# Two more first-layer units by seven products in chunks 2 and 3 of a fused attention and two-layer kernel

## The chip, the cores and the metric

The kernel runs on one core of a Trainium2 chip. The metric is the device time of one execution in microseconds. Before the change it is 325.47 us, the median of 3 runs (325.46 to 325.6). The engines are called PE (matrix products; PEld is its loading of weights), DVE (vector), ACT (activations), POOL (GpSimd) and SP (queue of transfers).

## The reference

Attention with a forgetting gate over 8 batches of 8 heads, 576 tokens and 64 values a head; its output, 4608 tokens of 512 values, goes through two layers with a gelu (tanh form) between them.

```
scores = q k^T / sqrt(64) + (cum[i] - cum[j]),  cum = cumsum(log(clip(f, 1e-4, 1)))
attn   = softmax over j <= i of scores;   x = attn v, heads side by side: 4608 x 512
out    = gelu_tanh(x @ w_in) @ w_out      w_in 512 x 2048, w_out 2048 x 512
```

## The kernel before

**Tiles.** A quad is four heads of one batch; there are 16, numbered 0 to 15, two in each batch. `xT` holds the attention output transposed, 512 values by 4608 tokens, and is filled by quads. The two layers go over the tokens in nine chunks (0 to 8) of 512. `gT` holds the gelus of the chunk at work.

**Stages.** FRONT, a string of words, covers the loads, quads 0 to 5, the layers of chunk 0 and most of chunk 1. Then TABLES[c] is played for chunks 2 to 8: first the rest of the chunk before (`O`), the first layer, and then the second layer woven with the attention of quads 2c+2 and 2c+3 and the first scores of 2c+4. In a table `q2` means quad 2c+2, and so on. The order is written by hand: each word issues its instructions to their engines, and each engine works through its own queue in that order.

**Words of attention** (a number after the dot is the quad). LK, LQ: load k, q on POOL's queue into one of two buffers (L192); LV: load values on SP's queue. TK, TQ: transpose them on DVE (L198). S.i.r: scores of round r on PE (L261) and their exponentials on ACT into `pt` (L269). M: causal masks by select on POOL (L275); m: masks by a product on DVE (L304). A last number picks the key block, so m.5.2.2 is quad 5, round 2, block 2. D: denominators on PE with the weights `w_bf` (L329), then two transposes and a reciprocal on DVE (L348 to L352). V.i.x: a half of the output on PE (L329) and its product on DVE into `xT` (L360). VW and vw: weighted values on POOL or DVE (L215). CL: copies a block of them (L220). D and V share one PSUM tile, `po`, which the DVE instruction behind each gives free. X and Y load the tables of ACT. D takes the key blocks in the order 0, low, 1, 2, 3, high.

**First layer.** P.n computes a pair of 128-row tiles of the 16 directly: 16 matmuls of 512 columns (L374) and one gelu (L381). P.n.1 takes the tile `po` for it. A unit by seven products (R.k, three words to a unit: `seven_in`, L412) computes the pairs k and k+4 together: seven products of 2 x 2 matmuls of 256 columns (L422), six sums and copies on DVE (L435 to L452), four gelus on ACT (L431). It takes two tiles `s` and both tiles `m` of PSUM. It needs four sums of the weights (K.k, L410; three are kept in the columns of an old chunk of `xT`, that of HOMES, the fourth, K.k.3, overwrites a part of `w_in_sb`) and four differences of the inputs (T, L395), which are kept in the columns of the chunk before in `xT`. So K.k.3 comes after the last direct use of these weights. In a table T makes the differences for the next chunk.

**Second layer.** G makes the sums of `gT` on DVE (L489 to L495). F and f pull so many of its 112 matmul steps (L510; f in four column strips). Its sums are L535 on DVE, its stores go on SP's queue.

**Units before.** Chunk 2 has no unit, chunk 3 one (k = 1), chunks 4 to 8 two (k = 1 and 3). All K are made in chunk 2, but for K.3.3 in chunk 3. Chunk 1 is played in the last three lines of FRONT (L80 to L82), with G.0, G.1.1.2 and the F and f of chunk 1; there V.4.1, CL.5 and m.5.2.2 stand next to each other, ahead of D.5.

Of the kernel before, what the change touches and what calls it, by code (L numbers as in the profile page):

```python
# [16 lines left out]
def kernel(  # L17
# [10 lines left out]
    nc = tc.nc  # L28

    B, H, S, D = q.shape  # L30
# [47 lines left out]
        J.0.2 J.1.2 X LK.4 F.0.6 TK.3 B.3.256 S.2.0 LK.5 F.0.9 S.2.2 F.0.10 S.2.1 TQ.3 TQ.4 F.0.10 LV.2.0@LK.5 m.2.1 vw.2 TK.4 S.3.0 f.0.1 M.2.2  # L78
        CL.2 LQ.5 M.2.0 D.2 f.0.6 S.3.1 m.3.0 F.0.6 V.2.0 S.3.2 TK.5 LK.6 M.3.2 f.0.7 V.2.1 CL.3 S.4.1 m.3.1 LQ.6 F.0.6 TQ.5 H.4.2.1 D.3 H.4.0.1
        LQ.7 VW.4 H.4.0.0 V.3.1 v.3.0 f.0.3 H.4.2.0 CL.4 I.1.0 m.4.1 U.0 LV.2.1@LQ.5 I.1.4 TQ.6 m.4.2.3 I.1.1 I.1.5 U.1 LV.3.0@LQ.7 LV.3.1 m.4.2.2  # L80
        TK.6 G.0 M.4.0 LK.7 LQ.8 LK.8 I.1.2 I.1.3 U.3 I.1.6 I.1.7 G.1.1.2 U.2 X F.1.16 S.5.0 f.1.26 S.5.1 D.4 M.5.0 f.1.16 S.5.2 V.4.0 m.5.2.3
        f.1.10 VW.5 V.4.1 CL.5 m.5.2.2 S.6.0 f.1.10 M.5.1 D.5 f.1.7 S.6.1 V.5.1 f.1.12 V.5.0 vw.6 S.6.2 m.6.1 M.6.2.2 m.6.0 m.6.2.3 CL.6  # L82
    """

    HOMES = {1: 0, 3: 1}
    TABLES = {}
    TABLES[2] = """
        Y O.512 P.0 P.1 TK.q3 TQ.q3 LK.q5 LQ.q5 TK.q4 TQ.q4 LK.q6 LQ.q6 LV P.4 P.5 G.0 P.2 P.3 P.6 P.7 G.1.1.2 X F.10 S.q3.0 D.q2 M.q3.0 f.22 S.q3.1
        V.q2.0 K.1.0 K.1.1 M.q3.1 VW.q3 f.18 S.q3.2 V.q2.1 M.q3.2 K.3.0 K.3.1 CL.q3 f.16 S.q4.0 VW.q4 D.q3 M.q4.0 f.18 S.q4.1 V.q3.0 K.1.2 K.1.3 K.3.2
        M.q4.1 f.9 V.q3.1 f.7 T CL.q4 S.q4.2  # L90
    """
    TABLES[3] = """
        Y O.512 P.0.1 R.1 P.4.1 R.1 R.1 TK.q3 TQ.q3 LK.q5 LQ.q5 M.q2.2 LV P.2 G.0 P.3 P.6 P.7 G.1.1.2 X F.10 S.q3.0 D.q2 M.q3.0 f.22 S.q3.1 V.q2.0
        K.3.3 TK.q4 TQ.q4 M.q3.1 VW.q3 f.18 S.q3.2 V.q2.1 M.q3.2 TK.q5 CL.q3 f.16 S.q4.0 VW.q4 D.q3 M.q4.0 f.18 S.q4.1 TQ.q5 V.q3.0 M.q4.1 f.13
        V.q3.1 T f.3 CL.q4 S.q4.2
    """
    TABLES[4] = """
        Y O.512 LK.q4 LQ.q4 P.0.1 R.1 P.4.1 R.1 R.1 LK.q5 LQ.q5 M.q2.2 LV R.3 P.2.1 R.3 G.0.1.2 P.6 R.3 G.0.3.4 G.1.1.2 X F.10 S.q3.0 D.q2 M.q3.0
# [28 lines left out]
    def many(n, shape, dtype, name):  # L127
        return [singles.tile(shape, dtype, name=f"{name}{i}") for i in range(n)]
# [11 lines left out]
    vw = many(2, [128, NT + 1, 4, D], BF16, "vw")  # L140
# [244 lines left out]
    def x_blocks(c):  # L385

        new, old = xT[:, :, CH * c:CH * (c + 1)], xT[:, :, CH * (c - 1):CH * c]
        return [z[:, 2 * a:2 * a + 2, HC * b:HC * (b + 1)] for z in (new, old) for a in range(2) for b in range(2)]

    def x_sums(c, which, eng):  # L390

        b11, b12, b21, b22, t1, t2, t3, t4 = x_blocks(c)
        todo = ((t1, b12, b11), (t2, b22, t1), (t4, b21, t2), (t3, b22, b12))
        for k in which:
            eng.tensor_sub(*todo[k])  # L395

    def w_blocks(k):

        n = 256
        a11, a12, a21, a22 = (w_in_sb[:, 2 * b:2 * b + 2, HU * a + n * k:HU * a + n * (k + 1)]  # L400
                              for a in range(2) for b in range(2))
        old = xT[:, :, CH * HOMES[k]:CH * (HOMES[k] + 1)]
        return a11, a12, a21, a22, old[:, 0:2, 0:n], old[:, 0:2, n:], old[:, 2:4, 0:n]

    def w_sums(k, eng, which):

        a11, a12, a21, a22, s1, s2, s4 = w_blocks(k)
        todo = ((s1, a21, a22), (s2, s1, a11), (s4, a12, s2), (a21, a11, a21))
        for n in which or range(4):
            (eng.tensor_sub if n else eng.tensor_add)(*todo[n])  # L410
# [246 lines left out]
    def out_part(c, n, tiled=0):  # L657
        by_columns[:] = [True] * tiled
        pull(fills.setdefault(c, seven_products(c) if c else mlp_out(c)), n)
# [5 lines left out]
    def load_values(b, half):  # L665
# [35 lines left out]
        "F": out_part,  # L701
        "f": lambda c, n: out_part(c, n, 1),
        "K": lambda k, *which: w_sums(k, nc.vector, which),
        "B": keep_busy,
        "X": load_exp,
        "Y": load_gelu,
# [81 lines left out]
```

## Time and profile before

| | us |
|---|---|
| median of 3 runs | 325.47 |
| the profiled execution | 325.69 |
| its span, from the first to the last instruction | 324.0 |
| PE busy | 312.9 |
| DVE busy | 242.2 |
| ACT busy | 202.8 |

The span is divided by the places in which PE starts a chunk's first layer: chunk 1 at 67.52, chunk 2 at 101.92, chunk 3 at 136.39, chunk 4 at 170.40, chunk 5 at 204.09, chunk 6 at 237.78. The groups of instructions that the change touches (columns: line, engine, operation, names, shapes, count; busy us and mean ns of one; idle us of the engine before them and what ended it):

```profile
L374 PE MATMUL ps_h<-xT,w_in_sb 128*128 128x512 bf16 x320 | 75.7, 379 | 0.8
L395 DVE TENSOR_TENSOR xT<-xT 128x512 bf16<-128x512 bf16 x24 | 9.6, 420 | 0.4
L435 DVE COPY snap<-ps_ab 128x512 f32<-128x512 f32 x11 | 7.6, 686 | 6.8 <-PE ps_ab L422 6.8
L304 DVE TENSOR_TENSOR pt<-pt,causal 128x512 bf16<-128x512 bf16 x12 | 6.2, 532 | 0.6 <-ACT pt L269 0.5
```

Matmuls are pipelined, so the 379 ns of one L374 overlap the next ones; what one costs is read from the stage that holds them. On DVE too the record of an instruction often overlaps the start of the next; the step from start to start is then what it costs.

### The profile page before, as it was taken

To read this page: it belongs to the slowest core of one execution; us is meant where nothing else is said; L and a number is where in the kernel's file an instruction comes from. 1 tells how busy PE (TensorE), PEld (TensorE's weight loads), DVE (VectorE), ACT (ScalarE), POOL (GpSimd) and SP (SyncE) were. 2 spreads that over 40 slices of the span, in tenths; PEclk is the share of its full clock that TensorE was granted. 3 is DMA by queue.
4 is the path that set the end of the run, shared out by engine and by line. 5 is a ranking of instruction groups with operands and counts; after the bars stand their busy time and mean duration, and the time that the engine had idled before them with its cause. 6 is when DMAs were issued, how large, how long until landed. Compare 5 with 4: busy or idle time off the path is not lost.

```text
span 324.0 us, 12192 instructions
## 1 busy us (share of the span) xinstructions
PE 312.9 (97%) x5479; PEld 214.5 (66%) x5499; DVE 242.2 (75%) x381; ACT 202.8 (63%) x245; POOL 107.8 (33%) x150
## 2 busy tenths in 40 slices
PE   3999999999999999999999999999999999999995
PEld 1357854544776467766777687667866786687684
DVE  5676138895769748978996899789977967885772
ACT  4585586776767677577657785678666842722630
POOL 8987554340320217302662047303720140000000
PEclk9999999999999999999999999999999999999999
DMA  7999999779201951285129611981120102012003
GB/s 130 204 208 209 194 225 203 151 142 234 58 4 67 220 108 36 67 177 79 36 66 182 149 36 36 166 195 38 36 67 0 35 15 89 0 35 97 3 32 99
DMA packets 46485, 33.45 MB, mean 103 GB/s; under 512 B 29792, under 2 KB 40160, under 8 KB 46432
## 3 DMA queue, kind: packets, MB, share of 16 engines
q0 software_dynamic: 8624, 15.99, 28.4%
q1 hardware_dynamic: 37664, 16.60, 19.4%
q8 instruction: 43, 0.70, 1.0%
q14 instruction: 10, 0.08, 0.1%
q10 hardware_dynamic: 144, 0.07, 0.1%
HBM read 36.85 MB, written 9.44 MB: 143 GB/s over the span
## 4 chain that ended last, share of the span: by engine, by line
PE 94%; POOL 2%; issue 1%; ACT 1%; DVE 1%; POOLq 0%; DVEq 0%; ACTq 0%
PE ps_w L510 30%; PE ps_h L374 22%; PE ps_s L261 10%; PE po L329 9%; PE ps_cd L422 6%; PE ps_ab L422 5%; PE ps_h L464 4%; PE pso L580 4%; PE po_m L315 1%; PE idle_ps L240 1%; ACT pt L269 1%; POOL v_nat L169 1%; PE ps_o L329 0%; DVE pt L304 0%; POOL q_c L192 0%
## 5 line engine op out<-in xcount | busy, mean ns | idle before, releaser
L269 ACT ACTIVATE pt<-ps_s 128x1024 bf16<-128x1024 f32 (+2 forms) x100 | 93.7, 988 | 36.9 <-PE ps_s L261 32.5
L275 POOL TENSOR_SCALAR_AFFINE_SELECT pt<-pt 128x512 bf16<-128x512 bf16 (+3 forms) x65 | 39.0, 610 | 117.5 <-ACT pt L269 116.5
L374 PE MATMUL ps_h<-xT,w_in_sb 128*128 128x512 bf16 x320 | 75.7, 379 | 0.8
L381 ACT ACTIVATE gT<-ps_h 128x1024 bf16<-128x1024 f32 x42 | 42.9, 1021 | 40.5 <-PE ps_h L374 40.1
L374 PEld LDWEIGHTS <-w_in_sb 128*128 128x128 bf16 x336 | 32.8, 98 | 34.6 <-issue 0.4
L510 PEld LDWEIGHTS <-gT 128*32 128x32 bf16 (+1 forms) x1247 | 50.7, 97 | 5.7 <-issue 1.7
L510 PE MATMUL ps_w<-w_out_sb,gT 128*32 128x256 bf16 (+1 forms) x1050 | 46.9, 273 | 0.0
L510 PEld LDWEIGHTS <-gsum 128*32 128x32 bf16 (+1 forms) x1256 | 39.1, 97 | 1.4
L261 PE MATMUL ps_s<-qT,kT 32*128 32x64 bf16 (+5 forms) x896 | 36.6, 265 | 0.1
L510 PE MATMUL ps_w<-usum,gsum 128*32 128x256 bf16 (+1 forms) x832 | 30.6, 273 | 0.0
L215 POOL TENSOR_TENSOR vw<-v_nat,wT 128x1280 bf16<-128x1280 f32 (+1 forms) x13 | 30.5, 2346 | 0.1
L198 DVE STREAM_TRANSPOSE kT<-k_c 128x576 f32<-128x576 f32 x16 | 19.9, 1244 | 14.1 <-DMA k_c<-in_k_dram 14.1
L535 DVE TENSOR_TENSOR o_st<-ps_w,snap 128x512 f32<-128x512 f32 x31 | 21.3, 690 | 10.5 <-PE ps_w L510 8.7
L261 PEld LDWEIGHTS <-kT 32*128 32x128 bf16 x896 | 16.6, 93 | 17.2 <-issue 12.3
L360 DVE TENSOR_TENSOR xT<-po,rb 128x576 bf16<-128x576 f32 x26 | 19.5, 751 | 5.9 <-PE po L329 5.4
L329 PE MATMUL po<-pt,vw 128*32 128x64 bf16 (+4 forms) x624 | 22.5, 279 | 0.0
L329 PEld LDWEIGHTS <-vw 128*32 128x32 bf16 x672 | 14.2, 97 | 10.5 <-issue 3.7
L422 PEld LDWEIGHTS <-w_in_sb 128*128 128x128 bf16 x176 | 17.2, 98 | 5.1 <-issue 0.8
L198 DVE STREAM_TRANSPOSE qT<-q_c 128x576 f32<-128x576 f32 x16 | 19.9, 1244 | 0.9 <-PE ps_s L261 0.7
L431 ACT ACTIVATE gT<-snap 128x512 bf16<-128x512 f32 x33 | 18.8, 623 | 0.7
L489 DVE TENSOR_TENSOR gsum<-gT 128x1024 bf16<-128x1024 bf16 x16 | 11.0, 685 | 11.1 <-ACT gT L381 11.1
L510 PE MATMUL ps_w<-usum,gT 128*128 128x256 bf16 (+1 forms) x197 | 16.9, 273 | 0.0
(100 smaller groups left out, 420.4 us busy)
## 6 DMA issues: line engine op xcount, KB each, us to landing
out_dram<-o_st SPq DMA_DIRECT2D x35, 256.0 KB, 2.3
k_c<-in_k_dram POOLq DMA_DIRECT2D x16, 288.0 KB, 5.5
q_c<-in_q_dram POOLq DMA_DIRECT2D x16, 288.0 KB, 6.9
v_nat<-in_v_dram SPq DMA_DIRECT2D x16, 256.0 KB, 6.1
v_nat<-in_v_dram SPq DMA_DIRECT2D x20, 128.0 KB, 4.9
w_in_sb<-in_moe_w_in_dram POOLq DMA_DIRECT2D x4, 512.0 KB, 10.0
w_out_sb<-in_moe_w_out_dram POOLq DMA_DIRECT2D x4, 512.0 KB, 8.8
v_nat<-in_v_dram POOLq DMA_DIRECT2D x9, 128.0 KB, 6.8
```

The source lines that it names most:

```text
L198: nc.vector.transpose(out=dst.rearrange("p s c -> p (s c)").bitcast(FP32) .rearrange("p (t a) -> p a t", a=S // 32), in_=src.rearrange("p ...
L215: eng.tensor_mul(vw[i % 2][:, t0:t1], vb[:, t0:t1, h0:h0 + 4, :], wT[:, i, t0:t1, :].unsqueeze(3).to_broadcast([128, t1 - t0, 4, D]))
L261: nc.tensor.matmul(tiles[h // 2][:, h % 2, c0:c0 + nq], key_columns(i, key, h, c), qq[32 * h:32 * h + 32, q0:q0 + nq, c], start=(c == 0 an ...
L269: nc.scalar.activation(p[:, 2 * g:2 * g + 2, off:off + n], t[:, :, 0:n], AF.Exp, scale=scale)
L275: nc.gpsimd.affine_select(out=x, in_=x, compare_op=ALU.is_ge, fill=0.0, base=0, pattern=pattern, channel_multiplier=-1)
L329: nc.tensor.matmul(po[r0:r0 + w.shape[-1], 448 + q0:448 + q0 + nq], w, p[:, h, col:col + nq], start=(key in (0, "low")), stop=(key in ("lo ...
L360: nc.vector.tensor_mul(xT[:, 2 * u + x, S * b + s0:S * b + s1], po, rbs[i, part])
L374: nc.tensor.matmul(ph[:, j, :], w_in_sb[:, dt, 128 * ft:128 * ft + 128], xT[:, dt, CH * c:CH * (c + 1)], start=(dt == 0), stop=(dt == N_DT ...
L381: nc.scalar.activation(gT[:, 2 * pr:2 * pr + 2, :], ph, AF.Gelu_apprx_tanh)
L422: nc.tensor.matmul(ps[:, j], w[:, dt, 128 * j:128 * j + 128], x[:, dt], start=(first and j == 0 and dt == 0), stop=(dt == 1), skip_group_c ...
L510: nc.tensor.matmul(ps[c0:c0 + width, n, cols[0]:cols[1]], x[:, j, 128 * n + c0:128 * n + c0 + width], w[:, j, cols[0]:cols[1]], start=(fir ...
L535: nc.vector.tensor_add(st, ps, kept[name])
```

## The change

Four edits to the tables and one word more in the front's list:

- FRONT: K.1.0 to 2 come after U.3, between the first-layer pairs of chunk 1; K.1.3 comes between V.4.1 and CL.5; T.2 (the differences for chunk 2) comes after V.5.0; vw.6 goes behind S.6.2. The masks of quad 6 (m.6.1, M.6.2.2, m.6.0, m.6.2.3) and CL.6 leave the front.
- Chunk 2: pairs 1 and 5 become a unit (R.1 three times). P.0 and P.4 take the tile `po`. The masks of quad 6 and CL.6 come after LQ.9. K.3.0 to 2 come after P.3 and K.3.3 after P.7; the K.1 words go. The transposes of quads 8 and 9 go into the second layer; the loads of quad 10 leave the chunk.
- Chunk 3: a second unit (R.3) in place of pairs 3 and 7, with the loads of quad 10 at the head; K.3.3 and the transposes of quad 9 leave it. The table is now word for word that of chunks 4 and 5.
- The word T is added to those that FRONT knows.

```diff
-        TK.6 G.0 M.4.0 LK.7 LQ.8 LK.8 I.1.2 I.1.3 U.3 I.1.6 I.1.7 G.1.1.2 U.2 X F.1.16 S.5.0 f.1.26 S.5.1 D.4 M.5.0 f.1.16 S.5.2 V.4.0 m.5.2.3
-        f.1.10 VW.5 V.4.1 CL.5 m.5.2.2 S.6.0 f.1.10 M.5.1 D.5 f.1.7 S.6.1 V.5.1 f.1.12 V.5.0 vw.6 S.6.2 m.6.1 M.6.2.2 m.6.0 m.6.2.3 CL.6
+        TK.6 G.0 M.4.0 LK.7 LQ.8 LK.8 I.1.2 I.1.3 U.3 K.1.0 K.1.1 K.1.2 I.1.6 I.1.7 G.1.1.2 U.2 X F.1.16 S.5.0 f.1.26 S.5.1 D.4 M.5.0 f.1.16 S.5.2
+        V.4.0 m.5.2.3 f.1.10 VW.5 V.4.1 K.1.3 CL.5 m.5.2.2 S.6.0 f.1.10 M.5.1 D.5 f.1.7 S.6.1 V.5.1 f.1.12 V.5.0 T.2 S.6.2 vw.6
...
     TABLES[2] = """
-        Y O.512 P.0 P.1 TK.q3 TQ.q3 LK.q5 LQ.q5 TK.q4 TQ.q4 LK.q6 LQ.q6 LV P.4 P.5 G.0 P.2 P.3 P.6 P.7 G.1.1.2 X F.10 S.q3.0 D.q2 M.q3.0 f.22 S.q3.1
-        V.q2.0 K.1.0 K.1.1 M.q3.1 VW.q3 f.18 S.q3.2 V.q2.1 M.q3.2 K.3.0 K.3.1 CL.q3 f.16 S.q4.0 VW.q4 D.q3 M.q4.0 f.18 S.q4.1 V.q3.0 K.1.2 K.1.3 K.3.2
-        M.q4.1 f.9 V.q3.1 f.7 T CL.q4 S.q4.2
+        Y O.512 P.0.1 R.1 P.4.1 R.1 R.1 TK.q3 TQ.q3 LK.q5 LQ.q5 m.q2.1 M.q2.2.2 m.q2.0 m.q2.2.3 CL.q2 LV P.2 G.0 P.3 K.3.0 K.3.1 K.3.2 P.6 P.7 K.3.3
+        G.1.1.2 X F.10 S.q3.0 D.q2 M.q3.0 f.22 S.q3.1 V.q2.0 TK.q4 TQ.q4 M.q3.1 VW.q3 f.18 S.q3.2 V.q2.1 M.q3.2 TK.q5 CL.q3 f.16 S.q4.0 VW.q4 D.q3
+        M.q4.0 f.18 S.q4.1 TQ.q5 V.q3.0 M.q4.1 f.13 V.q3.1 T f.3 CL.q4 S.q4.2
     """
     TABLES[3] = """
-        Y O.512 P.0.1 R.1 P.4.1 R.1 R.1 TK.q3 TQ.q3 LK.q5 LQ.q5 M.q2.2 LV P.2 G.0 P.3 P.6 P.7 G.1.1.2 X F.10 S.q3.0 D.q2 M.q3.0 f.22 S.q3.1 V.q2.0
-        K.3.3 TK.q4 TQ.q4 M.q3.1 VW.q3 f.18 S.q3.2 V.q2.1 M.q3.2 TK.q5 CL.q3 f.16 S.q4.0 VW.q4 D.q3 M.q4.0 f.18 S.q4.1 TQ.q5 V.q3.0 M.q4.1 f.13
-        V.q3.1 T f.3 CL.q4 S.q4.2
+        Y O.512 LK.q4 LQ.q4 P.0.1 R.1 P.4.1 R.1 R.1 LK.q5 LQ.q5 M.q2.2 LV R.3 P.2.1 R.3 G.0.1.2 P.6 R.3 G.0.3.4 G.1.1.2 X F.10 S.q3.0 D.q2 M.q3.0
+        f.22 S.q3.1 V.q2.0 TK.q4 TQ.q4 M.q3.1 VW.q3 f.18 S.q3.2 V.q2.1 M.q3.2 TK.q5 CL.q3 f.16 S.q4.0 VW.q4 D.q3 M.q4.0 f.18 S.q4.1 TQ.q5 V.q3.0
+        M.q4.1 f.13 V.q3.1 T f.3 CL.q4 S.q4.2
     """
...
+        "T": lambda c, *which: x_sums(c, which or range(4), nc.vector),
```

## The prediction, made before the changed kernel ran

> **What bounds the kernel now.** First the page: shares of busy time (columns: engine, busy us, share, instructions) and the chain that ended last.
>
> ```profile
> PE 312.9 (97%) x5479; PEld 214.5 (66%) x5499; DVE 242.2 (75%) x381; ACT 202.8 (63%) x245; POOL 107.8 (33%) x150
> ...
> PE 94%; POOL 2%; issue 1%; ACT 1%; DVE 1%; POOLq 0%; DVEq 0%; ACTq 0%
> ```
>
> PE is busy in 97% of the span and is 94% of the chain, so time changes only where PE gets less work or has to wait. Next I cut the span at PE's stage borders in the timeline (first L374 matmul of a chunk, first L510 matmul of its second layer) and asked for the busy times between them. Columns: stretch, its length, then busy us (instructions) of PE, PEld, DVE, ACT, POOL, clock, DMA share, GB/s.
>
> ```profile
> 101.92:115.73 13.81, 13.71 (x64) 6.27 (x64) 9.50 (x14) 9.06 (x10) 2.90 (x5) 1.00 0.82 164
> 115.73:136.39 20.66, 20.66 (x639) 15.90 (x638) 16.83 (x28) 14.29 (x17) 9.86 (x10) 1.00 0.18 47
> 136.39:149.81 13.42, 13.31 (x77) 7.44 (x77) 11.34 (x16) 9.41 (x12) 2.35 (x4) 1.00 0.80 158
> 149.81:170.40 20.59, 20.59 (x639) 15.86 (x638) 18.43 (x29) 14.28 (x17) 10.69 (x13) 1.00 0.21 53
> 170.40:183.58 13.18, 13.08 (x89) 8.61 (x89) 9.93 (x16) 9.25 (x14) 2.01 (x4) 1.00 1.03 199
> 183.58:204.09 20.51, 20.51 (x640) 15.73 (x638) 19.41 (x31) 14.67 (x18) 11.35 (x14) 1.00 0.16 44
> ```
>
> These are chunks 2, 3 and 4: first layer, then second layer with attention. The first layers differ in the number of seven-product units: none, one, two. So this profile already holds what the change makes of chunk 2 (chunk 3's table with one unit) and of chunk 3 (chunk 4's table, word for word). The clock is 1.00 throughout.
>
> **The change part by part.** The sum is made on the profiled execution: span 324.0 us, 325.69 us with what lies around it, 0.22 above the median 325.47. Differences are carried to the median unchanged.
>
> *Matmuls, chunk 2.* Two pair tiles (16 L374 matmuls of 512 columns) become one unit (28 L422 matmuls of 256). In chunk 2 the 64 matmuls take 13.81 us, 216 ns each: 16 are 3.45 us. The trace starts a group of four L422 matmuls every 0.44 us (138.12 to 139.87): seven groups 3.06 us. That is 0.39 less, and the measured stages give 13.42 - 13.81 = -0.39. The second layer takes chunk 3's form (20.59 against 20.66, with f.13 ahead of V instead of f.9): -0.07. Chunk 2: **-0.46**.
>
> *Matmuls, chunk 3.* One unit more: 13.18 - 13.42 = -0.24 (less than 0.39, as two units in one stage wait for the L435 copy and L452 sum between them). Second layer 20.51 - 20.59 = -0.08. Chunk 3: **-0.32**. The stages 204.09 to 217.26 (13.17) and 217.26 to 237.78 (20.52) repeat chunk 4 within 0.01.
>
> *What the units add off PE.* Each has six L435-L452 operations on DVE (0.69 us each: 4.1 us) and four L431 gelus of 0.6 on ACT instead of two L381 of 1.02 (+0.4). T.2 adds four L395 subtractions of 0.42 (1.67 us). These are inside the compared stages except where chunk 2's neighbours differ, so I walk DVE's queue there. Chunk 1's V.5.0 product starts on DVE at 99.82; T.2 from 100.49, 1.70 on; vw.6 1.40 (the step 100.50 to 101.90); the closing L535 from 103.59, the next instruction 0.61 later, 104.20. The unit's first copy in chunk 3 starts 138.76, 2.37 after the stage; in chunk 2 that is 104.29. DVE is free 0.09 us early: cost 0, because vw.6 and T.2 take the place of vw.6 and the three masks. With that cover gone each 0.1 us of lag delays the unit's third product (L440) by as much.
>
> *Weight sums in the front (K.1.0 to 2, before G.1.1.2).* Three L410 of 0.42 with 0.04 between: 1.4 us; at their slow rows (0.73 to 0.85, while POOL makes vw) 2.5. DVE ends U.3 at 79.63 and waits 3.03 us until 82.66 for the last gelu. Either fits: 0.
>
> *K.1.3 ahead of CL.5 and m.5.2.2.* Here something is late. DVE, columns start, us, instruction:
>
> ```profile
> 93.59 0.75 DVE L360 TENSOR_TENSOR xT<-po,rb 128x576 bf16<-128x576 f32 x1
> 94.38 0.22 DVE L220 COPY vw<-vw 64x256 bf16<-64x256 bf16 x1
> 94.61 0.42 DVE L304 TENSOR_TENSOR pt<-pt,causal 128x512 bf16<-128x512 bf16 x1
> 95.70 0.78 DVE L348 STREAM_TRANSPOSE den<-po 128x576 f32<-128x576 f32 x1 [0.67 <-PE po L329]
> ```
>
> The L304 is m.5.2.2, the mask that D.5 needs for key block 2. PE starts D.5 at 94.79, and by narrow windows its first 320-column matmul (block 2) at 95.22. How soon PE follows DVE is seen in chunk 4, where a group of L422 waits for its copy:
>
> ```profile
> 178.08 0.68 DVE L435 COPY snap<-ps_ab 128x512 f32<-128x512 f32 x1
> ```
>
> ```profile
> 178.22 0.60 PE L422 MATMUL ps_cd<-xT,w_in_sb 128*128 128x256 bf16 x4
> 178.82 0.60 PE L422 MATMUL ps_ab<-xT,w_in_sb 128*128 128x256 bf16 x4
> ```
>
> The copy ends at 178.76 and the next group, due 0.44 after 178.22, goes at 178.82: 0.06 after the copy. So the mask, ending 95.03, is in hand at 95.09, 0.13 ahead of need. K.1.3 stands before it. The like instruction, K.3.3 in chunk 3:
>
> ```profile
> 156.89 0.75 DVE L360 TENSOR_TENSOR xT<-po,rb 128x576 bf16<-128x576 f32 x1
> 157.56 0.41 DVE L410 TENSOR_TENSOR w_in_sb<-w_in_sb 128x512 bf16<-128x512 bf16 x1
> 157.89 1.25 DVE L198 STREAM_TRANSPOSE kT<-k_c 128x576 f32<-128x576 f32 x1
> ```
>
> pushes its follower by 0.33. 0.33 - 0.13 = **+0.20** of waiting in PE's queue, with all of PE's later work behind it. Bounds: 0, if the follower starts in some gap I cannot see; 0.85 - 0.13 = 0.72 at the slowest L410 row. POOL is idle from 91.28 to 102.43, so I take the fast row. D.5's transposes and V.5.1 only move along.
>
> *Chunk 2's end of the first layer on DVE.* Chunk 2 (34.47 us before chunk 3) now has chunk 3's unit, TK.7, TQ.7 and G.0, and besides them m.6.1, m.6.0, m.6.2.3, CL.6 and K.3.0 to 3. By chunk 3's rows: L452 at 108.99, TK.7 109.60, TQ.7 110.69, masks 111.77. Masks with CL.6 take 1.80 (101.90 to 103.70), G.0 2.75 (110.08 to 112.83), K.3.0 to 2 1.35, K.3.3 0.33 (P.7 is off PE by 115.34), G.1.1.2 1.56 (116.99 to 118.55), L348 of D.6 0.78: 120.34. V.6.0 needs that PSUM tile at 155.47 - 34.47 = 121.00, less 0.06: **0.60 us of margin**, cost 0. Late next, should it run out, are the first-corner L535 and V.6.0's own L360. The masks are due at D.6, near 117; done by 113.6. I bound this term by 0 and the 1.9 us of rival C.
>
> *DVE and POOL in that stretch.* In chunk 3 an L493 that needs 0.69 took 2.07 while POOL ran two selects:
>
> ```profile
> 146.95 2.07 DVE L493 TENSOR_TENSOR gT<-gT 128x1024 bf16<-128x1024 bf16 x1
> ...
> 147.23 1.23 POOL L275 TENSOR_SCALAR_AFFINE_SELECT pt<-pt 128x512 bf16<-128x512 bf16 x2
> ```
>
> and yet chunk 3 lost nothing on PE. Chunk 2 gets one select there (M.6.2.2, 0.6 to 0.8 us, after LQ.9 at 112.8), during the masks; the 1.80 for them comes from a stretch that holds such a select (102.43), so it is counted. The Trainium skill ("SBUF — State Buffer", "Who interferes with whom") says that a DVE instruction with two SBUF inputs and a GpSimd instruction that reads SBUF block each other whole, the later one waiting out the earlier. By it the select could come on top, up to 0.77 - 0.60 = 0.17 of stall, an estimate that makes the sum -0.41 instead of -0.58; the 2.07 row agrees with the rule.
>
> *Queues.* On POOL, LK.9 and LQ.9 wait for TK.7 and TQ.7 and are issued near 111.1 and 112.2, some 5 us later than before; they land in 5.5 and 6.9 us (page), and TK.9 is due only near 126.3, TQ.9 near 130.8. LK.10 and LQ.10 go from chunk 2 to the head of chunk 3, behind M.8.1 (POOL is free near 134); TK.10 is due near 157: 20 us of cover. Without it DVE would wait for a load, up to 7 us. M.6.2.2 is now queued behind LQ.9, due at 117. Behind it stand only masks of quad 7. On SP, LV.4 keeps its place after the stores. 0 for all of these.
>
> **Sum:** -0.46 - 0.32 + 0.20 = -0.58 us: 325.47 - 0.58 = **324.89** (span 323.4).
>
> **Rivals.**
> A. *No wait at D.5*: the mask is in time, say because CL.5 closes up behind K.1.3. For: 0.20 is a difference of small steps. Against: DVE runs in order, and L220 (94.38) started only after L360 had ended (94.34). 325.47 - 0.78 = 324.69.
> B. *Chunk 2's unit saves nothing*, so there the change doesn't do what it says: lag from T.2 and vw.6 reaches the unit. For: 0.09 us of room. Against: vw's 1.48 and the L395's 0.42 hardly vary without POOL. The 0.39 goes: 325.28.
> C. *DVE becomes the bound in chunk 2*: V.6.0 waits for D.6's L348. If one product meets POOL as in the 2.07 row (+1.38) and three K.3 sums take the slow rows (+0.38 each), DVE is 2.5 late: 2.5 - 0.60 = 1.9 of stall, 325.47 - 0.58 + 1.9 = 326.8. It eats the gain from 0.60 + 0.58 = 1.18 us of lag on. For: DVE has 18.6 us of work in the 20 us from T.2 to there (the terms above). Against: POOL has one select there and its vw products come after 123.
>
> **How the numbers follow.** Forecast 0.50, A 0.25, B 0.15, C 0.10. About 0.2% (0.65 us, 324.82) is what a measurement here can tell from no change. The forecast lies 0.07 inside it; of its 0.50 I give 0.12 to faster (a smaller stall), 0.38 to the same. A is faster. B is the same, C slower. Faster 0.37, same 0.53, slower 0.10. The range reaches from below A (324.69, less 0.09 of scatter between stages) past B, leaving out C: 324.6 to 325.5; the forecast's own is 324.75 to 325.05.
>
> **What would show it.** Chunk 2's first layer 13.4 us and chunk 3's 13.2, second layers 20.6 and 20.5; PE standing still about 0.2 us within D.5 near 95.2 with L304 of DVE as releaser (none: A); the first L435 of chunk 2 some 2.4 us after the stage's start (later: B); L348 of D.6 ending before V.6.0 is due (after: C). A wait of DVE for k_c or q_c, or of PE elsewhere in chunks 2 and 3, would make the forecast wrong.

## The result, and the profile after

The changed kernel takes 327.08 us (median of 5 runs, 326.67 to 327.17), the kernel before 325.47 (325.41 to 325.6, 5 runs on the same chip): ratio 1.0049, 95% interval 1.0035 to 1.0062. It is 1.6 us slower, half a per cent; the span of the profiled execution went from 324.0 to 325.4 us.

The page after: busy shares, and the chain that ended last by engine.

```profile
PE 312.7 (96%) x5503; PEld 216.6 (67%) x5523; DVE 250.5 (77%) x397; ACT 203.2 (62%) x249; POOL 106.9 (33%) x150
...
PE 87%; DVE 7%; POOL 2%; issue 2%; ACT 1%; POOLq 0%; DVEq 0%; ACTq 0%
```

DVE holds 7% of the chain where it had 1%: somewhere PE now waits for it. The stretches between PE's stage borders (columns as before: stretch, length, then busy us and instructions of PE, PEld, DVE, ACT, POOL, clock, DMA share, GB/s) say where:

```profile
81.40:102.08 20.68, 20.68 (x612) 15.86 (x611) 16.08 (x27) 14.52 (x17) 4.66 (x4) 1.00 0.16 47
102.08:115.50 13.42, 13.31 (x77) 7.44 (x77) 11.97 (x18) 9.18 (x12) 1.77 (x3) 1.00 0.75 142
115.50:138.14 22.64, 20.97 (x639) 15.85 (x638) 21.79 (x34) 14.29 (x17) 11.36 (x14) 1.00 0.20 42
138.14:151.31 13.17, 13.06 (x89) 8.60 (x88) 9.91 (x16) 9.24 (x14) 1.22 (x2) 1.00 0.94 205
151.31:171.81 20.50, 20.50 (x640) 15.72 (x638) 19.41 (x31) 14.67 (x18) 10.57 (x13) 1.00 0.16 44
```

| stretch | before | after | difference | forecast |
|---|---|---|---|---|
| chunk 1, second layer (81.40 to 101.92 before) | 20.52 | 20.68 | +0.16 | +0.20 |
| chunk 2, first layer | 13.81 | 13.42 | -0.39 | -0.39 |
| chunk 2, second layer | 20.66 | 22.64 | **+1.98** | -0.07 |
| chunk 3, first layer | 13.42 | 13.17 | -0.25 | -0.24 |
| chunk 3, second layer | 20.59 | 20.50 | -0.09 | -0.08 |
| sum | | | +1.41 | -0.58 |

The sum is the 1.4 us by which the two profiled executions differ. Four of the five came as forecast; one went wrong by 2.05 us. In that stretch the timeline of PE has two waits (columns: start, us, instruction, in brackets the idle time before it and who ended it):

```profile
130.99 0.62 PE L510 MATMUL ps_w<-w_out_sb,gsum 128*32 128x256 bf16 x16 [0.95 <-DVE o_st L535]
...
135.12 0.87 PE L329 MATMUL po<-pt,vw 128*32 128x512 bf16 x24 [0.73 <-DVE xT L360]
```

They are 1.68 us of idle time; the other 0.3 us of the loss lies in PE's records, which are longer there (20.97 us busy instead of 20.66).

DVE's timeline just before the first of them, and POOL's beside it:

```profile
126.89 1.24 DVE L198 STREAM_TRANSPOSE kT<-k_c 128x576 f32<-128x576 f32 x1
128.15 2.07 DVE L220 COPY vw<-vw 64x256 bf16<-64x256 bf16 x1
130.25 0.69 DVE L535 TENSOR_TENSOR o_st<-ps_w,snap 128x512 f32<-128x512 f32 x1
```

```profile
126.61 1.23 POOL L275 TENSOR_SCALAR_AFFINE_SELECT pt<-pt 128x512 bf16<-128x512 bf16 x2 [0.27 <-ACT pt L269]
127.81 2.33 POOL L215 TENSOR_TENSOR vw<-v_nat,wT 128x1280 bf16<-128x1280 f32 x1
```

The L220 is CL.7, a copy of 64 x 256 values. It takes 2.07 us, and its end, 130.22, lies 0.08 after the end of the L215 (VW.8) on POOL, 130.14. The two share no data: CL.7 needs VW.7, which had ended at 126.33. There is no idle time in front of the copy either, so what looks like a long copy is a wait inside it. In chunk 3 of the kernel before, whose form chunk 2 now has, the order was the other way round:

```profile
161.99 0.28 DVE L220 COPY vw<-vw 64x256 bf16<-64x256 bf16 x1
```

```profile
160.97 1.22 POOL L275 TENSOR_SCALAR_AFFINE_SELECT pt<-pt 128x512 bf16<-128x512 bf16 x2 [0.20 <-ACT pt L269]
162.17 2.33 POOL L215 TENSOR_TENSOR vw<-v_nat,wT 128x1280 bf16<-128x1280 f32 x1
```

There the copy came 0.18 us before POOL's product; it waited only for the end of the selects under way (162.20) and was done at 162.27. In the changed chunk 2 it comes 0.34 after it. (34.47 us earlier, and 0.17 later for D.5, chunk 3's copy would be wanted at 127.69: it is 0.46 late.)

### The profile page after: what moved, and what is told of

Same layout as the page of the kernel before. It is cut to its first block, busy times and chain, and to the rows that moved or that the text cites. A ratio compares the mean times of both kernels' runs of the same rounds, so it can differ in the third digit from the quotient of the medians.

```text
span 325.4 us, 12269 instructions
## 1 busy us (share of the span) xinstructions
PE 312.7 (96%) x5503; PEld 216.6 (67%) x5523; DVE 250.5 (77%) x397; ACT 203.2 (62%) x249; POOL 106.9 (33%) x150
## 4 chain that ended last, share of the span: by engine, by line
PE 87%; DVE 7%; POOL 2%; issue 2%; ACT 1%; POOLq 0%; DVEq 0%; ACTq 0%
PE ps_w L510 27%; PE ps_h L374 18%; PE ps_s L261 9%; PE po L329 9%; PE ps_cd L422 7%; PE ps_ab L422 6%; PE ps_h L464 4%; PE pso L580 4%; PE po_m L315 1%; PE idle_ps L240 1%; DVE pt L304 1%; ACT pt L269 1%; POOL v_nat L169 1%; DVE kT L198 1%; DVE vw L220 1%
## 5 line engine op out<-in xcount | busy, mean ns | idle before, releaser
L374 PE MATMUL ps_h<-xT,w_in_sb 128*128 128x512 bf16 x288 | 69.2, 379 | 0.8
L381 ACT ACTIVATE gT<-ps_h 128x1024 bf16<-128x1024 f32 x38 | 38.8, 1021 | 38.0 <-PE ps_h L374 37.4
L374 PEld LDWEIGHTS <-w_in_sb 128*128 128x128 bf16 x304 | 29.6, 98 | 30.2 <-issue 0.4
L215 POOL TENSOR_TENSOR vw<-v_nat,wT 128x1280 bf16<-128x1280 f32 (+1 forms) x13 | 30.3, 2334 | 0.1
L535 DVE TENSOR_TENSOR o_st<-ps_w,snap 128x512 f32<-128x512 f32 x31 | 21.3, 689 | 9.1 <-PE ps_w L510 7.6
L360 DVE TENSOR_TENSOR xT<-po,rb 128x576 bf16<-128x576 f32 x26 | 19.5, 751 | 4.7 <-PE po L329 4.2
L431 ACT ACTIVATE gT<-snap 128x512 bf16<-128x512 f32 x39 | 22.3, 623 | 0.8
L192 POOL DMA_DIRECT2D k_c<-in_k_dram x16 | 9.2, 577 | 27.8 <-DVE kT L198 22.4
L422 PEld LDWEIGHTS <-xT 128*128 128x128 bf16 x156 | 15.3, 98 | 4.5
```

Of the source, the lines that this page charges most:

```text
L215: eng.tensor_mul(vw[i % 2][:, t0:t1], vb[:, t0:t1, h0:h0 + 4, :], wT[:, i, t0:t1, :].unsqueeze(3).to_broadcast([128, t1 - t0, 4, D]))
L374: nc.tensor.matmul(ph[:, j, :], w_in_sb[:, dt, 128 * ft:128 * ft + 128], xT[:, dt, CH * c:CH * (c + 1)], start=(dt == 0), stop=(dt == N_DT ...
L381: nc.scalar.activation(gT[:, 2 * pr:2 * pr + 2, :], ph, AF.Gelu_apprx_tanh)
L422: nc.tensor.matmul(ps[:, j], w[:, dt, 128 * j:128 * j + 128], x[:, dt], start=(first and j == 0 and dt == 0), stop=(dt == 1), skip_group_c ...
L431: nc.scalar.activation(gT[:, ft:ft + 2, HC * j:HC * (j + 1)], x, AF.Gelu_apprx_tanh)
L535: nc.vector.tensor_add(st, ps, kept[name])
```

## The experiments

The edits are cut to the words that change and their neighbours. Two theories. **Theory 1, the order at a shared port:** a DVE copy from SBUF to SBUF cannot run while POOL runs an instruction that began before it; the extra work put ahead of it made CL.7 lose a race that it used to win. **Theory 2, overload:** chunk 2 has too much DVE work (21.79 us busy in 22.64, some 1.85 of them the wait inside the copy), and PE waits for that whatever POOL does. A third, that CL.7 waits for VW.8 as data, falls if the copy is ever short and done before VW.8.

### POOL's product later

```diff
-  TK.q5 CL.q3 f.16 S.q4.0 VW.q4 D.q3 M.q4.0 f.18
+  TK.q5 CL.q3 f.16 S.q4.0 D.q3 M.q4.0 VW.q4 f.18
```

> One word of chunk 2's table moves: VW.8, from before D.7 to behind the selects M.8.0. DVE's and PE's queues are not touched. Theory 1 (order at a shared port: the copy CL.7 on DVE, wanted at 128.15, waits out VW.8, which started on POOL at 127.81, so it takes 2.07 us instead of 0.22 and all of DVE's queue behind it is late): CL.7 finds POOL free, takes under 0.7 us, chunk 2's second layer falls from 22.64 to 20.6 us, and the time from 327.08 to about 325.0 (324.8 to 325.3). Theory 2 (overload: DVE has too much work in chunk 2, 21.79 us busy of 22.64, whatever POOL does): the same instructions, so no change, 326.8 to 327.2.

324.99 us (10 runs; before 325.52, ratio 0.9983, interval 0.9973 to 0.9993). DVE and then POOL:

```profile
128.23 0.22 DVE L220 COPY vw<-vw 64x256 bf16<-64x256 bf16 x1
```

```profile
126.68 1.23 POOL L275 TENSOR_SCALAR_AFFINE_SELECT pt<-pt 128x512 bf16<-128x512 bf16 x2 [0.27 <-ACT pt L269]
129.85 1.14 POOL L275 TENSOR_SCALAR_AFFINE_SELECT pt<-pt 64x256 bf16<-64x256 bf16 x2 [1.94 <-ACT pt L269]
131.07 2.34 POOL L215 TENSOR_TENSOR vw<-v_nat,wT 128x1280 bf16<-128x1280 f32 x1
```

The copy starts at the same place in DVE's queue and takes 0.22 us, as POOL is idle. No instruction of DVE or PE was moved, and some 2 us are back: chunk 2's second layer takes 20.79 us (115.58 to 136.37), 0.2 more than expected, for which no cause was sought. Theory 2 falls.

### The copy on another engine

```diff
-  TK.q5 CL.q3 f.16
+  TK.q5 cl.q3 f.16
+        "cl": lambda c, i: nc.scalar.copy(vw[i % 2][64:128, LOW], vw[i % 2][0:64, 0]),
```

> CL.7 in chunk 2 is made by ACT instead of DVE; VW.8 stays where it is. Theory 1: the copy never meets DVE's port, VW.8 holds up nothing, the time is about 325.0 (324.8 to 325.4). Theory 2: DVE has 0.2 us less to do, so at most 0.2 us is won, 326.8 to 327.1.

324.76 us (10 runs; ratio 0.9982, 0.9949 to 1.0014, so beside the kernel before unclear; against the change 2.3 us less, and just under theory 1's range). VW.8 runs where it did, from 127.81 for 2.33 us, and DVE beside it:

```profile
127.97 0.68 DVE L535 TENSOR_TENSOR o_st<-ps_w,snap 128x512 f32<-128x512 f32 x1
128.58 0.78 DVE L348 STREAM_TRANSPOSE den<-po 128x576 f32<-128x576 f32 x1
129.40 0.27 DVE L350 RECIPROCAL rec<-den 128x18 f32<-128x18 f32 x1
129.70 0.78 DVE L352 STREAM_TRANSPOSE rb<-rec 128x576 f32<-128x576 f32 x1
```

These four have their usual lengths beside POOL's product. So POOL's product does not slow DVE as a whole. Nor is the copy the only kind that it holds up: the two-input L493 of 2.07 us in the prediction and the slow L410 rows (0.73 to 0.85 us), all with their inputs in SBUF, were lengthened beside POOL as well. A copy from PSUM was not (L585 of the changed kernel, 0.68 us at 67.11 beside a select, 0.68 to 0.69 elsewhere).

### The same loss made in the kernel before

```diff
   (chunk 4 of the kernel before)
-  TK.q5 CL.q3
+  TK.q5 pad CL.q3
+    def pad():
+        words = idle.bitcast(FP32)
+        for _ in range(2):
+            nc.vector.transpose(out=words[:, 0:128], in_=words[:, 128:256])
```

> The kernel before, with two small DVE transposes (about 0.3 us each) on an idle tile put ahead of CL.9 in chunk 4. There CL wanted the port at 195.53 and the next VW started at 195.85. Theory 1: the copy now comes after 195.85 and waits until that VW ends (198.18): a copy of about 2 us and some 2 us more in all, 325.47 to 327.2 - 327.6. Theory 2: chunk 4's DVE has 19.41 us busy in 20.51, and 0.6 us more costs between 0 and 0.6 us: 325.4 to 326.1.

327.5 us (4 runs; ratio 1.006, 1.0045 to 1.0075). DVE, POOL and PE in chunk 4:

```profile
195.11 0.63 DVE L728 STREAM_TRANSPOSE idle<-idle 128x128 f32<-128x128 f32 x2
195.77 2.27 DVE L220 COPY vw<-vw 64x256 bf16<-64x256 bf16 x1
```

```profile
195.63 2.33 POOL L215 TENSOR_TENSOR vw<-v_nat,wT 128x1280 bf16<-128x1280 f32 x1
```

```profile
198.81 0.62 PE L510 MATMUL ps_w<-w_out_sb,gsum 128*32 128x256 bf16 x16 [1.00 <-DVE o_st L535]
...
202.94 0.87 PE L329 MATMUL po<-pt,vw 128*32 128x512 bf16 x24 [0.73 <-DVE xT L360]
```

0.63 us of harmless work cost 2.0 us. The copy was 0.14 us late and took 2.27 us, against 0.34 late and 2.07 in the change: its length is what is left of POOL's product, and the two waits of PE behind it are the same two. Chunk 4's second layer went to 22.61 us.

### Less work ahead of the copy

```diff
-  P.3 K.3.0 K.3.1 K.3.2 P.6 P.7 K.3.3 G.1.1.2
+  P.3 K.3.0 K.3.1 P.6 P.7 G.1.1.2
...
-  V.q3.0 M.q4.1
+  V.q3.0 K.3.2 K.3.3 M.q4.1
```

> The change, with K.3.2 and K.3.3 moved from chunk 2's first layer to behind V.7.0: about 0.8 us less on DVE ahead of CL.7, the same work in the chunk. Theory 1: CL.7 is wanted near 127.4, before VW.8 starts at 127.81, takes under 0.7 us; the later sums can delay V.7.1's product a little, as they did before the change (20.66): 325.0 to 325.3. Theory 2: the chunk's DVE work is the same, so the loss stays or shrinks by no more than the 0.8 us: 326.3 to 327.1.

324.81 us (10 runs; ratio 0.9977, 0.9967 to 0.9986), a little below theory 1's range.

```profile
127.35 0.55 DVE L220 COPY vw<-vw 64x256 bf16<-64x256 bf16 x1
```

```profile
126.59 1.23 POOL L275 TENSOR_SCALAR_AFFINE_SELECT pt<-pt 128x512 bf16<-128x512 bf16 x2 [0.27 <-ACT pt L269]
127.79 2.33 POOL L215 TENSOR_TENSOR vw<-v_nat,wT 128x1280 bf16<-128x1280 f32 x1
```

All of DVE's work is still in the chunk, in another order. The copy, there at 127.35, waits for the selects under way, is done at 127.90, and POOL's product, recorded from 127.79, runs on. The copy was done 2.2 us before VW.8 ended, so it did not need VW.8's data: the third theory falls too.

### The copy still later

```diff
-  TK.q5 CL.q3 f.16 S.q4.0 VW.q4 D.q3 M.q4.0
+  TK.q5 f.16 S.q4.0 VW.q4 D.q3 CL.q3 M.q4.0
```

> The change with CL.7 put four instructions later on DVE, behind D.7's transposes (wanted near 130.3 instead of 128.15); VW.8 as in the change ends at 130.14. Theory 1: a copy that comes later is shorter, 0.2 to 1.1 us (POOL's two small selects run until 131.2), and the L535 and D.7's L348 no longer stand behind it: 325.0 to 325.6. Theory 2: order on DVE doesn't matter, and a later CL.7 can only make V.7.0 later: 327.0 to 327.6.

325.05 us (10 runs; before 325.75 in this set; ratio 0.998, 0.9957 to 1.0003). VW.8 ran from 127.38 to 129.71, and

```profile
130.08 0.22 DVE L220 COPY vw<-vw 64x256 bf16<-64x256 bf16 x1
```

Four instructions later in DVE's order, the copy takes 0.22 us instead of 2.07. It came between POOL's two selects: seen in narrow windows, the first is recorded from 129.66 for 0.41 us, so until 130.07, and the second from 130.14. The second layer took 20.8 us, 0.2 above the best, from V.7.1 a little late.

### Chunk 2's unit taken out

```diff
-  V.4.1 K.1.3 CL.5 m.5.2.2      (front)     V.5.0 T.2 S.6.2 vw.6
+  V.4.1 CL.5 m.5.2.2            (front)     V.5.0 S.6.2 vw.6
-  P.0.1 R.1 P.4.1 R.1 R.1 TK.q3 TQ.q3
+  P.0.1 P.1 P.4.1 P.5 K.1.3 TK.q3 TQ.q3
```

> The change without chunk 2's unit: pairs 1 and 5 direct, no T.2, K.1.3 after pair 5; chunk 3 keeps its second unit. DVE has about 6 us less to do in chunk 2. Theory 1: CL.7 is wanted well before VW.8 starts and is short; first layer 13.8, second layer 20.6 us; chunk 3 13.2 and 20.5; no wait in D.5: 325.47 - 0.07 - 0.32 = 325.1 (324.9 to 325.3). If chunk 3's second unit had a cost of its own that the change's loss hides, it shows here as 325.5 or more.

325.14 us (10 runs; ratio 0.998, 0.9971 to 0.9989). By PE's timeline the stages are 13.81 (101.91 to 115.72) and 20.59, chunk 3's 13.18 and 20.50. CL.7 came at 127.58, 0.44 us ahead of VW.8, and took 0.54. Chunk 3's second unit is worth its 0.3 us and has no hidden cost.

### Both repairs

The edit of "Less work ahead of the copy", and besides

```diff
-  V.4.1 K.1.3 CL.5 m.5.2.2 S.6.0
+  V.4.1 CL.5 m.5.2.2 K.1.3 S.6.0
```

> The kernel of two_sums_later with K.1.3 also moved behind m.5.2.2, so that D.5's mask is made at its old time. If the wait of 0.17 us inside D.5 in the change is K.1.3's alone, chunk 1's second layer goes from 20.68 back to 20.52 us and D.5's 24 matmuls close up: span 323.1 to 323.2, time 324.5 to 324.8. If that wait has another cause, it stays and the span is 323.3. Against the kernel before this is the whole gain of the two units, -0.78 us forecast.

324.53 us (6 runs; before 325.75; ratio 0.9975, 0.9958 to 0.9991). Chunk 1's second layer and chunk 2's two stages:

```profile
81.14:101.66 20.52, 20.52 (x612) 15.92 (x611) 16.07 (x27) 14.52 (x17) 4.66 (x4) 1.00 0.15 46
101.66:115.08 13.42, 13.42 (x79) 7.43 (x76) 11.97 (x18) 9.18 (x12) 1.77 (x3) 1.00 0.78 140
115.08:135.68 20.60, 20.60 (x640) 15.81 (x639) 20.16 (x34) 14.30 (x17) 11.51 (x14) 1.00 0.20 50
```

PE is busy through all three. D.5, first in the change and then here:

```profile
94.79 1.03 PE L329 MATMUL po<-pt,w_bf 128*32 128x512 bf16 x24
```

```profile
94.54 0.86 PE L329 MATMUL po<-pt,w_bf 128*32 128x512 bf16 x24
```

The 0.17 us inside D.5 were K.1.3's, and the stage is back at 20.52. This kernel is faster than the kernel before and than the change. Its median is the lowest of the study, but the 0.28 us to the kernel with the two sums alone lie within what the runs of one kernel differ by. (Its span, 322.9, is 0.25 below what the stages explain: chunk 1 starts up to 0.5 us earlier or later from one kernel's profile to the next, its first L374 matmul between 67.10 and 67.61, by nothing that the edits touch. Stage lengths are the better measure for tenths.)

### One number in all the traces

In the nine traces, 42 of the L220 copies began while POOL was in a select or product that had begun earlier. They took 0.26 to 2.27 us, and every one of them ended 0.08 us after that one instruction of POOL (0.076 to 0.083). A transfer that POOL was issuing (L192) did not hold a copy up like this: the changed kernel's copy at 172.10 took 0.22 beside one.

## Why the prediction was wrong

**Right, with sizes.** What bounds the kernel, the price of a unit in each chunk (-0.39, -0.25), the wait of D.5 (+0.20 forecast, 0.17 measured; K.1.3 pushed the mask's end from 95.03 to 95.34), the weight sums hidden in the front (G.1.1.2's L489 at 82.65, as before) and the two ends of DVE's walk through chunk 2's first layer: the unit's first copy 2.37 us after the stage's start, as forecast, and D.6's L348 at 119.80, forecast 119.56 plus D.5's 0.17. That the second end fits is partly luck: the masks with CL.6 took 2.21 us where 1.80 was counted (one L304 lasted 1.27 beside the select), and the sums behind them 0.34 less than counted. V.6.0 did not wait. Rivals A and B did not happen. (A pair P.n is 8 matmuls, as the 64 of eight pairs show, not the 16 given with the kernel; the prediction's count of 16 for two pairs is right.)

**The step that failed** is "The second layer takes chunk 3's form (20.59 against 20.66, with f.13 ahead of V instead of f.9): -0.07". It carried over a stage's length from chunk 3, but not the state in which DVE enters it. The walk of the queue was stopped at V.6.0, where it found 0.60 us of margin, and I wrote that "Late next, should it run out, are the first-corner L535 and V.6.0's own L360". But DVE entered the second layer later than chunk 3's did, and a smaller margin stood further on: 0.18 us between CL and POOL's product in chunk 3. DVE was 0.46 late there. The prediction's own numbers come near it: its L348 at 119.56 is 1.40 later than chunk 3's (152.63 less 34.47); 0.56 goes into DVE's idle time ahead of chunk 3's first L535 (at 155.08), and 0.33 is K.3.3, which chunk 2 no longer has at this place; 0.5 is left. The runs put in place of -0.07 a +1.98, of which the collision is 2.04 (22.64 against 20.60 without it).

**Rival C** had the kind of mechanism, DVE late and a product of POOL's in the way, and its size (1.9 us of stall; this is chance, as C added up other instructions), but another place, and it was turned down with the very thing that decided: "POOL has one select there and its vw products come after 123". It looked for a meeting up to V.6.0 only. Its point of decision, 1.18 us of lag, was wrong also: the price was no gradual one; 0.46 us of lag cost 2.0 us at once. That the range left out all of C was the second error.

The rule weighed in the prediction from the Trainium skill ("SBUF — State Buffer", "Who interferes with whom") has a sentence next to the one I used, that a `copy` whose operands meet the conditions can enter a mode that takes the shared ports as well, and that the one that issues first blocks the other whole. By it the copy ends when VW.8 does: 130.14, measured 130.22. The trace agrees, and DVE's transposes beside VW.8 (0.78 each) kept their usual length. That it is this mode of the copy which takes the port was not tried here; shown is that the copy waits out POOL's product, and that the four other DVE instructions beside it do not. The prediction's own row, the L493 of 2.07 us, fits the rule that it weighed only in part: the L493 is recorded from 146.95, ahead of the selects (147.23), and yet it is the one that got longer, while the selects kept their 0.64 us each. What it waited for is open.

## What to carry to other kernels

When work is put ahead of an instruction, follow the queue to the next place where the lag is absorbed, and at each DVE copy on the way look at what POOL runs then: here a copy within SBUF that came 0.18 us ahead of POOL's long product took 0.28 us, and those that came 0.14 and 0.34 us after its start took what was left of it, 2.27 and 2.07. In a trace such a wait has no idle time and no releaser; it shows as one instruction much longer than its like. Where a stage's time is taken over from another chunk, take over the margins at its start as well.

## What was not expected of the hardware

- A copy of the same size took 0.22, 0.28, 0.55, 2.07 and 2.27 us, by what POOL was doing and since when; those that met POOL at work ended 0.08 us after it.
- A copy that waits for a select got its turn before POOL's next queued instruction was done (there at 127.35, done at 127.90, POOL's product 127.79 to 130.12), and that product was not longer for it (2.33).
- Making a copy later (128.15 to 130.08) made the kernel 2 us faster.
